# Reordering the last stage of a one-core decode kernel: value products around a layer norm, w_out in two transfers, the last value pieces re-cut

## The chip, the cores and the metric

The kernel runs on one core of a Trainium2 chip. A core has five instruction streams that meet only through semaphores: TensorE (PE, matrix products, with the weight loads shown as PEld), VectorE (DVE), ScalarE (ACT), GpSimd (POOL) and SyncE (SP, which here issues nearly every transfer). The transfers themselves run on 16 DMA engines. The metric is the device time of one execution in microseconds (us); of several executions the median is taken.

## The reference

Four sequences (B = 4) each decode one token. The input row is normalised and modulated, goes through attention over a cache of 4096 keys and values in 32 heads of 128, and then through a gated mixer.

```
mod = silu(c) @ w_mod                       # six groups of 512: sa, ca, ga, sb, cb, gb
h = layernorm(x) * (1 + ca) + sa
q = (h @ wq) in 32 heads of 128
p = softmax(q . k_cache * 128 ** -0.5)      # 4096 keys per head and sequence
x = x + ga * ((p . v_cache) @ wo)
h = layernorm(x) * (1 + cb) + sb
z = gelu(h @ w_in)                          # 1792 columns, two halves of 896
g = w_sp * layernorm(z[second half]) + b_sp # w_sp, b_sp are one number each
x = x + gb * ((z[first half] * g) @ w_out)
```

All inputs are bf16. The two caches together are 256 MiB, and each byte of them is read once, so nearly all of the time is the time of streaming them.

## The kernel before

**Tiles.** The work on the caches is cut into 32 tiles (`NT`), each 4 heads of one sequence: 128 slots (`NJ`) of 128 numbers on each of 128 partitions, 4 MiB of keys and 4 MiB of values. Thirty of them are handled as pairs. The last two (`N0` = 30 and `L` = 31) are single tiles, the last eight heads of the last sequence (`BL` = 3). For each tile the keys are multiplied by the query on DVE (`mult`), summed over the head's dimension on PE and DVE (`reduce_d`, `sum8`, `sum_rest`), and turned into exponentials on ACT (`exps`), which land in `pbd8`. The values then meet these weights on PE (`pv`): groups of four slots are the moving operand, 512 columns, and four groups run side by side in four column strips of the array.

**Buffers and transfers.** Three SBUF buffers of 64 KB per partition (`bufA`, `bufB`, `bufC`) take keys and values in turn. When the keys are through, the weights of the second half of the block are loaded into `bufA`. SP issues, in this order and after the last paired value tile is used: the values of tile `N0` into `bufC` (4 MiB, one transfer), the values of tile `L` into `bufB` in the pieces of `TAIL` (32, 32, 32, 16, 16 slots of 32 KB each), `w_in` in two transfers (`KIN`), `w_out` in one, and the `gb` columns of `w_mod` in two (`KG`, three quarters and one quarter). All are on one hardware queue.

**Order of work.** The order on every engine is the order of the program text (a manual schedule); each engine works through its own list and waits where an operand isn't there. There is no planner that moves work.

**The last stage.** It begins after the loop over the tiles. `turn()` finishes the projection by `wo` of everything but the last eight heads of the last sequence and turns it into columns. DVE then makes `acc` (L777) and `x1` (L779), the row with the attention of all finished heads added. `normed` (L231) is the layer norm over it: a copy, a sum across partitions on PE (`across`, L219), the subtraction, the square, a second `across`, a sum on DVE and ACT's reciprocal root. It has two hooks, `then` and `last`, by which a caller can put PE work behind the first and ahead of the second `across`. Before the change neither is used here.

After it, for the two single tiles: `pv(N0)` (L513, 32 matmuls) makes four partial roots which `o_pick` (L522, L526, four DVE instructions) picks out and adds, `o_cols` (L538) turns into a column, and `o_scale` (L561) scales into `oTp`. `deal` and `dealt` (L640, L652, L658) spread that column for the projection. The last tile `L` goes by pieces, `o_last(L, part)`: pieces 0 and 1 (8 matmuls each) as `pv` does into the other accumulator `ops`, picked by `o_pick(L)`; pieces 2, 3 and 4 slot by slot with the values as stationary operand (L549), into one small accumulator `qps`. `o_first(L)` (L555) adds the picked part of pieces 0 and 1 into the same accumulator. `o_proj4` (L617) and `o_proj` (L607) project the two tiles. The layer norm is then corrected for this one sequence (L801 to L831), and the mixer follows: `gate` (L852), GELU, `zz`, `y` (L877, 28 matmuls by `w_out`), `gb` (L885, 16 matmuls), the mixer's own norm (L890 to L908), the sums of L905 to L918, a transposition (L920) and the output.

Of the kernel before, what the change touches and what calls it, by code (L numbers as in the profile page):

```python
# [9 lines left out]
F32 = mybir.dt.float32  # L10
AF = mybir.ActivationFunctionType
ALU = mybir.AluOpType
AX = mybir.AxisListType
# [3 lines left out]
HP = 8  # L17
KC = 64
RD = 8
TAIL = (32, 32, 32, 16, 16)  # L20
KIN = (slice(0, 2), slice(2, 4))
KG = (slice(0, 3), slice(3, 4))


class Arena:
# [24 lines left out]
def kernel(  # L50
# [16 lines left out]
    nc = tc.nc  # L67
    P = 128
    B, _, D = A_x.shape
# [3 lines left out]
    DJ = D // P  # L73
    NF = F // P
    NH = FH // P
    NJ = SK * HQ // P
    NP = 2 * NJ
    R = P // HQ
    G = 4
    NT = B * H // HQ  # L80
    GP = H // HP - 1
    N0 = NT - 2
# [6 lines left out]
    L = NT - 1  # L89
# [88 lines left out]
    def spread(n, pattern, axis, **sizes):  # L178
# [18 lines left out]
        out=far, in0=half, scalar1=-1.0, scalar2=-NEG, op0=ALU.add, op1=ALU.mult  # L197
    )
    nc.vector.tensor_scalar(
        out=fars, in0=far[:, :, None].to_broadcast([P, 2, R // 2]), scalar1=-1.0, scalar2=None, op0=ALU.mult  # L200
# [30 lines left out]
    def normed(pool, src, name, then=None, last=None):  # L231

        sb = pool.tile([P, B, DJ], F32, name=f"sb_{name}")
        nc.vector.tensor_copy(out=sb, in_=src.rearrange("p j b -> p b j"))
        m = across(sb, inv_d)
        if then:
            then()
        m = summed(pool, m, f"m_{name}")
        xc = pool.tile([P, DJ, B], F32, name=f"xc_{name}")
        nc.vector.tensor_tensor(out=xc, in0=src, in1=bc(m, DJ), op=ALU.subtract)  # L240
        sq = pool.tile([P, B, DJ], F32, name=f"sq_{name}")
        xb = xc.rearrange("p j b -> p b j")
        nc.vector.tensor_tensor(out=sq, in0=xb, in1=xb, op=ALU.mult)
        if last:
            last()
        v = summed(pool, across(sq, inv_d), f"v_{name}")
        rs = pool.tile([P, B], F32, name=f"rs_{name}")
        rsqrt(rs, v, 1.0, eps)
        return xc, rs
# [6 lines left out]
        out=sg, in0=cx, scalar1=-60.0, scalar2=-1.0, op0=ALU.max, op1=ALU.mult  # L256
# [6 lines left out]
    def mod_cols(s0, n, dst):  # L263
# [20 lines left out]
        out=hs, in0=modA[:, DJ:2 * DJ, :], scalar=1.0, in1=xn, op0=ALU.add, op1=ALU.mult  # L284
# [55 lines left out]
    g8 = consts.tile([P, 2, B], F32, name="g8")  # L340
# [163 lines left out]
    def pv(i):  # L504
        n = (NP if pair(i) else NJ) // G
        pv_some(i, 0, n, n)

    def pv_some(i, m0, m1, end):
        pb, vt, rows = (pbd8, bufC, G * HP) if pair(i) else (pbds[:, i % 4], vts[i], G * HQ)
        for m in range(m0, m1):  # L510
            n = slice(m * G, (m + 1) * G)
            g = R * (m % 4)
            nc.tensor.matmul(  # L513
                ops_of(i)[g:g + rows], lhsT=pb[:, n, :], rhs=vt[:, n, :],
                start=(m < 4), stop=(m >= end - 4), tile_position=(0, g),
            )

    def o_pick(i):
        ops = ops_of(i)
        sel = sels[HP if pair(i) else HQ]  # L520
        osb = wk.tile([P, DH], F32, name="osb", bufs=2)
        nc.vector.tensor_scalar(  # L522
            out=osb, in0=ops[:, 0, :], scalar1=sel[:, 0:1], scalar2=None, op0=ALU.mult
        )
        for g in range(1, G):
            nc.vector.scalar_tensor_tensor(  # L526
                out=osb, in0=ops[:, g, :], scalar=sel[:, g:g + 1], in1=osb,
                op0=ALU.mult, op1=ALU.add,
            )
        st[i, "osb"] = osb  # L530

    def o_cols(i):
        if pair(i):
            op = ps_sm([P, P])
            nc.tensor.transpose(op, st.pop((i, "osb")), ident_f)
        else:
            op = ps_sm([P, HQ])
            nc.tensor.matmul(op, lhsT=st.pop((i, "osb")), rhs=sel4, start=True, stop=True)  # L538
        st[i, "op"] = op

    def o_last(i, part):
        n0, n1 = sum(TAIL[:part]), sum(TAIL[:part + 1])
        if part < 2:
            pv_some(i, n0 // G, n1 // G, sum(TAIL[:2]) // G)
            return
        if part == 2:
            st[i, "op"] = psum.tile([P, HQ], F32, name="qps", bufs=1)
        for k in range(n0, n1):
            nc.tensor.matmul(  # L549
                st[i, "op"], lhsT=vts[i][:, k, :], rhs=pbds[:, i % 4, k, :],  # L550
                start=(part == 2 and k == n0), stop=(k == NJ - 1),
            )

    def o_first(i):
        nc.tensor.matmul(st[i, "op"], lhsT=st.pop((i, "osb")), rhs=sel4, start=False, stop=False)  # L555
# [25 lines left out]
    wout_sb = Arena(bufA, 46 * KB, 53 * KB).tile([P, NH, D], BF16)  # L581
    wg_sb = Arena(bufA, 53 * KB, 57 * KB).tile([P, DJ, D], BF16)
    late = Arena(bufA, 57 * KB, 64 * KB)
    tl = Arena(bufC, 32 * KB, 64 * KB)
# [11 lines left out]
    def load_end():  # L596
        win = B_w_in.rearrange("(p j) n -> p j n", p=P)
        for ks in KIN:
            nc.sync.dma_start(out=win_sb[:, ks], in_=win[:, ks])
        nc.sync.dma_start(out=wout_sb, in_=B_w_out.rearrange("(j p) n -> p j n", p=P))  # L600
        for ks in KG:
            nc.sync.dma_start(out=wg_sb[:, ks], in_=wm[:, ks, 5 * D:])

# [44 lines left out]
    def dealt(k, b0=0):  # L648
        pp = st.pop(("pp", k, b0))
        n, nb = pp.shape[1], pp.shape[2]  # L650
        ow = own if n == HP else own[:, 0:n * nb, 0:n]
        nc.vector.tensor_tensor(  # L652
            out=ow, in0=pp.rearrange("p r b h -> p (r b) h"),
            in1=bc(mask8 if n == HP else mask4, n * nb), op=ALU.mult,
        )
        od = late.tile([P, n, nb], BF16, name=f"od{k}{b0}")
        with nc.allow_low_precision("all but one term of each sum are zero"):
            nc.vector.tensor_reduce(  # L658
                out=od.rearrange("p r b -> p (r b)"), in_=ow, axis=AX.X, op=ALU.add
            )  # L660
        st["od", k, b0] = od
# [106 lines left out]
    for i in (N0, L):  # L768
        norm_a(i)
    nc.vector.tensor_reduce(  # L770
        out=sel32, in_=ident_f.rearrange("p (q r) -> p r q", r=R), axis=AX.X, op=ALU.add
# [5 lines left out]
    nc.vector.tensor_tensor(out=acc, in0=wp, in1=gaT, op=ALU.mult)  # L777
    x1 = x1w[:, :, 0:B]
    nc.vector.tensor_tensor(out=x1, in0=acc, in1=xT, op=ALU.add)  # L779
    xc, rs2 = normed(tl, x1, "ln2")  # L780
    pv(N0)
    o_last(L, 0)
    o_pick(N0)
    o_cols(N0)
    o_scale(N0)
    o_last(L, 1)
    deal(GP, slice(BL, B))
    dealt(GP, BL)
    o_pick(L)
    o_last(L, 2)  # L790
    o_first(L)
    wp = ps_sm([P, DJ, 1])
    for j in range(DJ):
        o_proj4(wp, j, slice(BL, B), j == 0)
    o_last(L, 3)
    o_last(L, 4)
    o_scale(L)
    for j in range(DJ):
# [16 lines left out]
        out=x1m, in0=x1[:, :, :, None].to_broadcast([P, DJ, B, HQ]),  # L815
        in1=mask4[:, None, None, :].to_broadcast([P, DJ, B, HQ]), op=ALU.mult,
# [4 lines left out]
        out=nv2, in0=mq2[:, 0:1], scalar=mq2[:, 0:1], in1=mq2[:, 1:2],  # L821
# [7 lines left out]
        out=hl, in0=xs, scalar=mq2[:, 0:1], in1=cbT[:, :, BL], op0=ALU.subtract, op1=ALU.mult  # L829
    )  # L830
    nc.vector.scalar_tensor_tensor(  # L831
        out=hT2[:, :, BL], in0=hl, scalar=rsl, in1=sbT[:, :, BL], op0=ALU.mult, op1=ALU.add
# [3 lines left out]
    for k in range(DJ):  # L836
        nc.tensor.matmul(
            x1r[:, k:P:DJ], lhsT=x1m[:, k].rearrange("p b j -> p (b j)"), rhs=sel32,
            start=True, stop=True,
# [6 lines left out]
    def gate(h, part):  # L846
# [22 lines left out]
    zz = tl.tile([P, NH, 2, B], BF16, name="zz")  # L869
    nc.vector.tensor_tensor(  # L870
        out=zz.rearrange("p f g b -> p g b f"), in0=z1[:, None].to_broadcast([P, 2, B, NH]),
        in1=st3[:, 0:2], op=ALU.mult,
    )
    y = ps_q()[:, 0:DJ * 2 * B].rearrange("p (j g b) -> p j g b", j=DJ, g=2)
    for j in range(DJ):
        for f in range(NH):
            nc.tensor.matmul(  # L877
                y[:, j], lhsT=wout_sb[:, f, j * P:(j + 1) * P], rhs=zz[:, f],
                start=(f == 0), stop=(f == NH - 1),
            )  # L880

    gb = ps_sm([P, DJ, B])
    for k in range(DJ):
        for j in range(DJ):
            nc.tensor.matmul(  # L885
                gb[:, j, :], lhsT=wg_sb[:, k, j * P:(j + 1) * P], rhs=cT[:, k, :],
                start=(k == 0 and j == 0), stop=(k == DJ - 1), skip_group_check=True,
# [3 lines left out]
        out=mq3, in_=ps3.rearrange("p (g b f) -> p g b f", g=2, b=B), axis=AX.X, op=ALU.add  # L891
    )
    rs3 = tl.tile([P, B], F32, name="rs3")
    nc.vector.tensor_tensor(out=rs3, in0=mq3[:, 0], in1=mq3[:, 0], op=ALU.mult)
    nc.vector.scalar_tensor_tensor(
        out=rs3, in0=mq3[:, 1], scalar=LN_EPS, in1=rs3, op0=ALU.add, op1=ALU.subtract
# [5 lines left out]

    yb = y.rearrange("p j g b -> p g b j")
    t3 = tl.tile([P, 3, B, DJ], F32, name="t3")
    nc.vector.tensor_scalar(  # L905
        out=t3[:, 2], in0=yb[:, 0], scalar1=spf[:, 1:2], scalar2=None, op0=ALU.mult
    )
    nc.vector.tensor_tensor(  # L908
        out=g8, in0=g8, in1=rs3[:, None, :].to_broadcast([P, 2, B]), op=ALU.mult
    )  # L910
    nc.vector.tensor_tensor(
        out=t3[:, 0:2], in0=g8[:, :, :, None].to_broadcast([P, 2, B, DJ]), in1=yb, op=ALU.mult
    )
    tt = tl.tile([P, B, DJ], F32, name="tt")
    nc.vector.tensor_reduce(
        out=tt, in_=t3.rearrange("p g b j -> p b j g"), axis=AX.X, op=ALU.add
    )
    nc.vector.tensor_tensor(out=tt, in0=tt, in1=gb.rearrange("p j b -> p b j"), op=ALU.mult)  # L918
    rows = ps_sm([B * DJ, P])
    nc.tensor.transpose(rows, tt.rearrange("p b j -> p (b j)"), ident_f)  # L920
# [33 lines left out]
```

## Time and profile before

| | |
|---|---|
| runs | 665.11, 665.56, 667.5 us; median 665.56 us |
| profiled execution | 667.08 us |
| its span, first to last instruction | 665.0 us |
| DVE busy | 571.1 us (86%) |
| PE matmuls busy | 318.1 us (48%) |
| ACT busy | 171.3 us (26%) |
| POOL busy | 20.0 us (3%) |
| HBM read | 282.73 MB, 425 GB/s over the span |
| mean granted TensorE clock | 0.744 |

The engines work beside each other, so their busy times don't add up to the span. The profile is one execution, and its own time is 2.08 us above its span. Times "at 641.18" are microseconds from the span's start. The chain of waits is the path that set the end: at each step what released it.

### The profile page before, as it was taken

What the parts mean: (1) busy time and instruction counts of PE and PEld (TensorE: products, weight loads), DVE (VectorE), ACT (ScalarE), POOL (GpSimd) and SP (SyncE); (2) the same over time, 40 slices, a digit from 0 to 9 for tenths busy, and PEclk for the clock granted to TensorE, in tenths of its full rate; (3) what the DMA queues carried; (4) which work ended last, traced back from release to release, by engine and by line L of the source; (5) the groups of instructions that cost most, each with busy time, mean ns of one, the idle gap of its engine ahead of it and who ended that gap; (6) DMA issues with size and microseconds to landing.
All of it is one profiled execution on the core that took longest, in us unless ns stands there. A gap on an engine that the chain in (4) does not pass through costs nothing.

```text
span 665.0 us, 5225 instructions
## 1 busy us (share of the span) xinstructions
PE 318.1 (48%) x2134; PEld 137.4 (21%) x2134; DVE 571.1 (86%) x403; ACT 171.3 (26%) x284; POOL 20.0 (3%) x57
## 2 busy tenths in 40 slices
PE   1563543646152364625246461434646243465885
PEld 0221111212021121202112120211212021122344
DVE  3259999989898998989899897989989898999823
ACT  1210606032050604205060410506032050605212
POOL 3000000000000000000000000000000000003100
PEclk9988787857677786767778676787867578787865
DMA  8999999999999999999999999999999999999995
GB/s 362 451 431 430 441 435 442 435 442 435 434 410 441 435 430 441 435 438 439 422 434 442 422 427 441 438 438 442 422 434 435 430 434 439 416 437 430 425 411 205
DMA packets 9356, 283.07 MB, mean 426 GB/s; under 512 B 876, under 2 KB 2804, under 8 KB 3956
## 3 DMA queue, kind: packets, MB, share of 16 engines
q1 hardware_dynamic: 9312, 282.73, 98.6%
q8 instruction: 16, 0.26, 0.1%
q14 instruction: 8, 0.07, 0.0%
q10 hardware_dynamic: 20, 0.01, 0.0%
HBM read 282.73 MB, written 0.00 MB: 425 GB/s over the span
## 4 chain that ended last, share of the span: by engine, by line
DMA 60%; DVE 17%; PE 17%; ACT 4%; issue 1%; POOL 0%; SPq 0%; DVEq 0%; ACTq 0%
DMA bC<-in_A_v_cache_dram 44%; DMA bA<-in_A_k_cache_dram 12%; PE ops L513 10%; DVE bA L384 7%; DVE S L404 5%; ACT pbd L458 3%; PE red L392 3%; DMA bC<-in_w_mod_dram 3%; DVE bB L384 1%; DVE S L415 1%; DMA bC<-in_B_b_sp_dram 1%; PE sm L670 1%; PE qps L319 1%; DVE osb L526 1%; PE sm L311 1%
## 5 line engine op out<-in xcount | busy, mean ns | idle before, releaser
L458 ACT ACTIVATE pbd<-S,nb 32x256 bf16<-32x256 f32 x120 | 154.2, 1519 | 424.9 <-DVE nb L445 423.7
L384 DVE TENSOR_TENSOR bA<-bA,qbp 128x8192 bf16<-128x8192 bf16 x32 | 141.1, 4411 | 25.3 <-DMA bA<-in_A_k_cache_dram 25.3
L392 PE MATMUL red<-bB,ident_bf 128*128 128x512 bf16 x344 | 97.2, 442 | 116.4 <-DVE bB L384 116.3
L392 PE MATMUL red<-bA,ident_bf 128*128 128x512 bf16 x332 | 94.0, 443 | 113.6 <-DVE bA L384 113.4
L392 PEld LDWEIGHTS <-ident_bf 128*128 128x128 bf16 x676 | 73.2, 110 | 344.2 <-issue 176.2
L384 DVE TENSOR_TENSOR bB<-bB,qbp 128x8192 bf16<-128x8192 bf16 x28 | 123.7, 4417 | 15.0 <-DMA bB<-in_A_k_cache_dram 15.0
L513 PE MATMUL ops<-bC,pbd 128*32 128x512 bf16 (+1 forms) x992 | 88.4, 534 | 70.3 <-DMA bC<-in_A_v_cache_dram 65.3
L404 DVE TENSOR_REDUCE S<-bA 128x48 f32<-128x6144 bf16 x15 | 98.1, 6541 | 0.0
L404 DVE TENSOR_REDUCE S<-bB 128x48 f32<-128x6144 bf16 x14 | 91.6, 6542 | 0.0
L513 PEld LDWEIGHTS <-pbd 128*32 128x32 bf16 (+1 forms) x1008 | 37.4, 128 | 119.9 <-issue 65.1
L458 ACT ACTIVATION_READ_ACCUMULATOR pbd<-S,nb 32x1 f32 x120 | 58.6, 489 | 0.0
L415 DVE TENSOR_REDUCE S<-red 128x64 f32<-128x512 f32 x64 | 43.7, 683 | 4.3 <-PE red L392 4.3
L472 POOL TENSOR_TENSOR rsb<-maskd,rs 128x8 f32<-128x8 f32 x15 | 3.9, 260 | 581.3 <-ACT pbd L458 581.3
L384 DVE TENSOR_TENSOR bB<-bB,qbo 128x8192 bf16<-128x8192 bf16 x4 | 17.6, 4412 | 0.0
L526 DVE SCALAR_TENSOR_TENSOR osb<-ops,m,osb 128x128 f32<-128x128 f32 x45 | 15.8, 351 | 1.6
L491 PE MATMUL sm<-rsb,inv_d 128*128 128x32 f32 (+2 forms) x12 | 3.1, 356 | 15.2 <-POOL rsb L472 14.4
L458 ACT ACTIVATE pbd<-S,nM 32x128 bf16<-32x128 f32 x8 | 4.6, 576 | 13.7 <-POOL pbd L718 12.5
L283 DVE SCALAR_TENSOR_TENSOR bC<-sm,bC 128x16 f32<-128x16 f32 x1 | 0.2, 173 | 8.5 <-PE sm L269 8.5
L428 DVE TENSOR_REDUCE mrow<-S 128x1 f32<-128x256 f32 (+1 forms) x17 | 6.9, 404 | 0.6
L631 POOL COPY bA<-ident_bf 128x1024 bf16<-128x1024 bf16 (+1 forms) x2 | 6.5, 3272 | 0.0
L319 PE MATMUL qps<-bC 128*128 128x256 bf16 (+1 forms) x16 | 4.5, 383 | 4.1 <-ACT qbp L329 2.8
L360 DVE COPY modT<-sm 128x48 f32<-128x48 f32 x1 | 0.2, 208 | 7.0 <-PE sm L357 7.0
(160 smaller groups left out, 139.5 us busy)
## 6 DMA issues: line engine op xcount, KB each, us to landing
bA<-in_A_k_cache_dram SPq DMA_DIRECT2D x2, 4096.0 KB, 32.1
bC<-in_A_wq_dram SPq DMA_DIRECT2D x1, 4096.0 KB, 12.2
bB<-in_A_k_cache_dram SPq DMA_DIRECT2D x1, 4096.0 KB, 41.5
bB<-in_A_k_cache_dram SPq DMA_DIRECT2D x2, 2048.0 KB, 40.8
bC<-in_A_v_cache_dram SPq DMA_DIRECT2D x1, 4096.0 KB
bA<-in_A_wo_dram SPq DMA_DIRECT2D x3, 1024.0 KB, 36.8
bB<-in_A_v_cache_dram SPq DMA_DIRECT2D x3, 1024.0 KB, 17.4
bC<-in_w_mod_dram SPq DMA_DIRECT2D x1, 2560.0 KB, 17.9
```

Source lines behind the costliest of these rows:

```text
L311: nc.tensor.matmul(qr[R * q:R * (q + 1)], lhsT=hT[:, k, :], rhs=wq_v[:, k, gs, q, :], start=(k == 0), stop=(k == DJ - 1), tile_position=(0 ...
L319: nc.tensor.matmul(qp[:, 0:npair], lhsT=eb2[k][:, b].rearrange("p k q r -> p (k q r)"), rhs=qrow[:, h, k:2 * npair:2], start=(k == 0), sto ...
L384: nc.vector.tensor_tensor(out=kt, in0=kt, in1=bc(q, KC), op=ALU.mult)
L392: nc.tensor.matmul(red, lhsT=ident_bf, rhs=kt[:, :, m * rd:(m + 1) * rd], start=(m == 0), stop=(m == DH // rd - 1),)
L404: nc.vector.tensor_reduce(out=st[i, "S"][:, n0:NJ], in_=kts[i][:, n0:NJ, :], axis=AX.X, op=ALU.add)
L415: nc.vector.tensor_reduce(out=st[i, "S"][:, kc * KC:kc * KC + on_pe(i, kc)], in_=st.pop((i, "red", kc)), axis=AX.X, op=ALU.add,)
L428: nc.vector.tensor_reduce(out=mrow, in_=S, axis=AX.X, op=ALU.max)
L458: nc.scalar.activation(out=pbd8[r, :, 2 * q + h] if pair(i) else pbds[r, i % 4, :, q], in_=S[r, :], func=AF.Exp, bias=nM[r, h:h + 1], scal ...
L513: nc.tensor.matmul(ops_of(i)[g:g + rows], lhsT=pb[:, n, :], rhs=vt[:, n, :], start=(m < 4), stop=(m >= end - 4), tile_position=(0, g),)
L526: nc.vector.scalar_tensor_tensor(out=osb, in0=ops[:, g, :], scalar=sel[:, g:g + 1], in1=osb, op0=ALU.mult, op1=ALU.add,)
L631: nc.gpsimd.tensor_copy(out=picks[n].rearrange("p r (a u) -> p r a u", a=n), in_=ident_bf.rearrange("p (u r) -> p r u", r=n)[:, :, None, : ...
L670: nc.tensor.matmul(wp, lhsT=od[:, r, :], rhs=wo_sb[:, k * HP + r, :], start=(k == 0 and r == 0), stop=(k == GP - 1 and r == HP - 1),)
```

## The change

Seven edits, all in the last stage or in its transfers.

1. `TAIL` ends in pieces of 24 and 8 slots where it had 16 and 16.
2. `w_out` is loaded in two transfers, the first four and the last three of its seven row blocks (`JW`), where it had one.
3. `pv(N0)` is cut in three: 8 matmuls before the layer norm, 16 behind its first `across` and 8 ahead of its second, where all 32 stood behind the norm.
4. `o_last(L, 1)` stands ahead of `o_cols(N0)`; it stood behind `o_scale(N0)`. `o_last(L, 2)` stands ahead of `o_pick(L)`, where it stood behind it; the two are on different engines.
5. `o_first(L)` stands between `o_last(L, 3)` and `o_last(L, 4)`; it stood before the projection `o_proj4`.
6. The matmuls of `y` go through the first four row blocks of `w_out` for all four groups of columns, and then through the last three, with one start flag for the whole accumulator.
7. At the end the factor `rs3` of the mixer's norm is applied to a sum of two terms, where it was applied to the coefficients `g8`; a three-term reduction becomes two additions.

```diff
-TAIL = (32, 32, 32, 16, 16)
+TAIL = (32, 32, 32, 24, 8)
+JW = (slice(0, 4), slice(4, 7))
...
-        nc.sync.dma_start(out=wout_sb, in_=B_w_out.rearrange("(j p) n -> p j n", p=P))
+        wout = B_w_out.rearrange("(j p) n -> p j n", p=P)
+        for js in JW:
+            nc.sync.dma_start(out=wout_sb[:, js], in_=wout[:, js])
...
-    xc, rs2 = normed(tl, x1, "ln2")
-    pv(N0)
+    nv = NJ // G
+    pv_some(N0, 0, nv // 4, nv)
+    xc, rs2 = normed(
+        tl, x1, "ln2",
+        lambda: pv_some(N0, nv // 4, 3 * nv // 4, nv), lambda: pv_some(N0, 3 * nv // 4, nv, nv),
+    )
     o_last(L, 0)
     o_pick(N0)
+    o_last(L, 1)
     o_cols(N0)
     o_scale(N0)
-    o_last(L, 1)
     deal(GP, slice(BL, B))
     dealt(GP, BL)
+    o_last(L, 2)
     o_pick(L)
-    o_last(L, 2)
-    o_first(L)
     wp = ps_sm([P, DJ, 1])
     for j in range(DJ):
         o_proj4(wp, j, slice(BL, B), j == 0)
     o_last(L, 3)
+    o_first(L)
     o_last(L, 4)
...
-    for j in range(DJ):
-        for f in range(NH):
-            nc.tensor.matmul(
-                y[:, j], lhsT=wout_sb[:, f, j * P:(j + 1) * P], rhs=zz[:, f],
-                start=(f == 0), stop=(f == NH - 1),
-            )
+    for js in JW:
+        for j in range(DJ):
+            for f in range(NH)[js]:
+                nc.tensor.matmul(
+                    y[:, j], lhsT=wout_sb[:, f, j * P:(j + 1) * P], rhs=zz[:, f],
+                    start=(j == 0 and f == 0), stop=(f == NH - 1), skip_group_check=True,
+                )
...
     t3 = tl.tile([P, 3, B, DJ], F32, name="t3")
+    nc.vector.tensor_tensor(
+        out=t3[:, 0:2], in0=g8[:, :, :, None].to_broadcast([P, 2, B, DJ]), in1=yb, op=ALU.mult
+    )
     nc.vector.tensor_scalar(
         out=t3[:, 2], in0=yb[:, 0], scalar1=spf[:, 1:2], scalar2=None, op0=ALU.mult
     )
+    tt = tl.tile([P, B, DJ], F32, name="tt")
+    nc.vector.tensor_tensor(out=tt, in0=t3[:, 0], in1=t3[:, 1], op=ALU.add)
     nc.vector.tensor_tensor(
-        out=g8, in0=g8, in1=rs3[:, None, :].to_broadcast([P, 2, B]), op=ALU.mult
-    )
-    nc.vector.tensor_tensor(
-        out=t3[:, 0:2], in0=g8[:, :, :, None].to_broadcast([P, 2, B, DJ]), in1=yb, op=ALU.mult
-    )
-    tt = tl.tile([P, B, DJ], F32, name="tt")
-    nc.vector.tensor_reduce(
-        out=tt, in_=t3.rearrange("p g b j -> p b j g"), axis=AX.X, op=ALU.add
-    )
+        out=tt, in0=tt, in1=rs3[:, :, None].to_broadcast([P, B, DJ]), op=ALU.mult
+    )
+    nc.vector.tensor_tensor(out=tt, in0=tt, in1=t3[:, 2], op=ALU.add)
     nc.vector.tensor_tensor(out=tt, in0=tt, in1=gb.rearrange("p j b -> p b j"), op=ALU.mult)
```

## The prediction

> **What bounds the kernel now.** I read the page first: busy shares, the chain, and the slices for the transfers. The whole span is a stream from HBM, and then a last stretch that is not.
>
> ```profile
> span 665.0 us, 5225 instructions
> ...
> PE 318.1 (48%) x2134; PEld 137.4 (21%) x2134; DVE 571.1 (86%) x403; ACT 171.3 (26%) x284; POOL 20.0 (3%) x57
> ...
> DMA 60%; DVE 17%; PE 17%; ACT 4%; issue 1%; POOL 0%; SPq 0%; DVEq 0%; ACTq 0%
> ```
>
> DVE is busy for 86%, but transfers hold 60% of the chain. The change touches nothing before 640 us, so I went to the chain of waits there (start, length, what):
>
> ```profile
> 641.18 0.19 DVE bA L777
> ...
> 643.20 0.61 PE sm L219 x2
> 643.80 3.55 PE ops L513 x30
> ...
> 649.03 0.35 PE sm L538 x2
> 649.39 0.54 PE ops L513 x8
> 649.93 0.20 PE sm L640 x4
> ...
> 654.01 0.17 DVE oTp L561
> ...
> 661.77 0.18 DVE bC L918
> ```
>
> From 641.18 on no transfer stands in the chain: it is PE and DVE handing small results to each other, with PE idle in the layer norm (641.15 to 643.73, but for two `across`) and behind each `o_pick`. What these idle stretches are worth is the question. Third, SP's timeline, for the transfers (start, issue time):
>
> ```profile
> 640.69 0.38 SPq L600 DMA_DIRECT2D bA<-in_B_w_out_dram  x1
> 643.13 9.28 SPq L602 DMA_DIRECT2D bA<-in_w_mod_dram  x2
> ```
>
> SP's waits say that L600 waited for the values of `N0` and L602 for the first piece of `L`'s, so these landed at 640.69 and 643.13. `w_out` is the ninth transfer from `N0`'s values on and waits for the first; the tenth waits for the second. Fourth, stretches of the last stage (length, PE, PEld, DVE, ACT, POOL busy, clock, DMA share, GB/s):
>
> ```profile
> 641.42:644.83 3.41, 2.24 (x16) 1.40 (x20) 1.06 (x6) 0.50 (x2) 0.33 (x2) 0.50 1.01 425
> 644.84:648.25 3.41, 3.34 (x32) 0.87 (x24) 0.80 (x3) 0.00 (x0) 0.31 (x2) 0.50 1.01 416
> 648.25:651.66 3.41, 1.89 (x46) 1.38 (x46) 2.13 (x9) 0.00 (x0) 0.00 (x0) 1.00 1.02 419
> ...
> 656.00:658.00 2.00, 1.29 (x32) 1.20 (x33) 0.94 (x5) 1.31 (x3) 0.00 (x0) 0.50 0.61 210
> ```
>
> The queue is full until about 655 and ends near 658.1; the clock is half in two of the first three stretches.
>
> **When data lands.** Value pieces of `L`: the first at 643.13; the fourth was issued at about 627.2 and took 22.2 us, so 649.4. That is 2.5 MiB in 6.27 us, 2.5 us a MiB: piece 1 at 645.6, piece 2 at 648.1, and everything at 650.6. `w_in` 631.0 + 23.8 = 654.8. `w_mod`'s first piece 643.13 + 15.1 = 658.2; its second, 128 KB at some 200 GB/s, 658.9. `w_out` lies between 654.8 and 658.2, 896 of 1280 KB: 657.2, and its first 512 KB 656.2. These are estimates but for the landings that a row shows.
>
> **A, `pv(N0)` around the norm.** 32 matmuls move ahead; they issue no transfer, and their values are there (640.69) before the turned projection ends (641.15). Four run in 0.43 us at half clock (32 took 3.59). Eight go into 641.05 to 641.95, while DVE makes `acc`, `x1` and the copy, ready at 641.84: the first `across` starts at 641.95 in place of 641.90. The other 24 follow from 642.5 and take 2.57, so 645.1 with 0.17 to drain. The price: the second `across` stands behind them, and DVE's sum of it stands ahead of `o_pick(N0)`; 645.2 + 0.61 + 0.05 + 0.18, and `o_pick` begins at 646.05, ends 1.52 later at 647.57, where it ended at 648.90. ACT's root and POOL's L810 wait 2 us longer, but L811's result is first used at 657.4. Gain 1.33 at half clock. If the clock returns to full at 644.83, the rest of `pv` is over at 645.07, `across` takes 0.3 (at full clock L491 does two such sums in 0.58) and `o_pick` ends at 647.14: gain 1.76.
>
> Whether it returns is open. The flips of the clock that I narrowed down (638.0, 648.25, 651.66) are whole multiples of 3.41 apart; a stretch with 3.25 of 3.41 us of 512-column matmuls (504.89 to 508.30) was followed by full clock, one with 2.19 (566.33 to 569.74) was not. The new 641.42 to 644.83 has about 2.8. It lies as near to one as to the other, so I keep both ends. The Trainium skill ("TensorE: Matmul & The Clock Gate", Part 1) says the same of windows: they are free-running, 3413 ns long, and a busy one brings the full rate. By that page alone the full-clock values here and below would stand, and the whole gain would be 2.4 to 2.7; going by half clock it is 2.2. The flips agree with its length; no row shows its threshold.
>
> **B, `o_last(L, 1)` ahead of `o_cols(N0)`.** Now the wait from `o_pick`'s end to the end of `deal` is 648.90 to 650.13, 1.23, because `deal` stands behind eight matmuls (0.54). They move into `o_pick`'s time (PE is free from about 645.8, piece 1 is there at 645.6). What is left: 0.13 + 0.35 + 0.05 + 0.17 + 0.04 + 0.22 = 0.96, or 1.20 if `o_cols` runs at half clock (L555, the same shape, took 0.59). Gain 0.27 or 0.03. `deal` ends at 648.10 or 648.77. What now waits behind piece 1 on PE is `o_cols`, and behind that all of the chain: a piece 2 us late would cost directly.
>
> **C, `o_first` late, pieces 24 and 8.** Now from `deal`'s end to L561: 3.88 (650.13 to 654.01), because `o_first` waits for `o_pick(L)` with 16 + 32 short matmuls behind it. After: piece 2 (0.92), `o_proj4` (0.52), 24 of piece 3 (0.65), `o_first` (0.59), 8 of piece 4 (0.32 with the drain), 0.04: 3.0. `o_pick(L)` ends 1.83 after `deal`, inside that. At half clock L561 starts at 648.77 + 3.0 = 651.8, gain 2.2. At full clock `deal` is so early that piece 3 (24 slots, landing at 649.4 + 0.6 = 650.0) holds PE: 650.0 + 0.65 + 0.59 (or 0.35) + 0.32 + 0.04 = 651.6 (651.35), gain 2.4 (2.65). Without the cut at 24 the wait would be no shorter: all slots land at 650.6 in both.
>
> **D, the tail.** L801 to L870 move as a block. `y` would start at 659.74 - 2.4 = 657.34: its first blocks are there at 656.2, the rest at 657.2 and used 0.5 later. `gb`'s last four matmuls need 658.9, and the product by it stands at 661.77 - 2.4 = 659.37: covered by about 0.3. If this cover goes, the end is 658.9 + 0.2 and the gain is limited to 2.7. The new sums: from `y` ready (660.65) five DVE steps, 0.22 + 0.26 + three of 0.20, end at 661.73 before the last product, where it starts at 661.77 now. Removing `g8`'s product and the reduction saves 0.4 behind `rs3`, but the two terms of `y` have moved behind `y`. 0.0, between 0.1 either way. The start flag and the loop order of `y` cost nothing: 28 matmuls before and after.
>
> **E, `w_out` in two.** One more issue on SP (0.38), ahead of `w_mod`'s. The second half waits for piece 0 (643.13), `w_mod` for pieces 1 and 2 (645.6, 648.1); but its issue took 6.59 and 2.65 us and ended at 649.7 and 652.4, so these waits lie inside it. 0, if the issue's end is set by the queue draining; the rivals price the other case.
>
> **Sum.** 2.2 at half clock to 2.7 at full: I take 2.4, since both ends depend on a threshold that no row gives. Span 665.0 to 662.6; the profiled execution 667.08 to 664.7. That execution lies 1.5 above the median, 665.56, and from the median it is 663.2.
>
> **Rivals.**
> *Transfers take it back.* The last rows of `w_mod`, in 1 KB rows, went at 210 GB/s, not 405. If both parts of `w_out` (917 kB, also 1 KB rows) go at 210, everything behind them lands 4.4 - 2.3 = 2.1 us later, `gb` ends at about 661.2, and only 0.5 us is left: 665.0. Value pieces 1 us late (B, C) would give 664.2. For it: 0.91 and 0.61 of DMA share where the last pieces are alone. Against: two value pieces of 512 KB ran at a share of 1.0. The Trainium skill ("DMA: Bandwidth & Descriptors", Rules for kernel authors) asks for at least 1 MiB a transfer, which speaks against cutting `w_out`; the 512 KB pieces here don't bear that out.
> *Slower: SP holds the last weights.* `w_out`'s second part has 384 rows of 1 KB, as the `w_mod` piece has whose issue took 6.59 us. If that is the issue's own price, SP passes `w_out` at 649.7, the `w_mod` pieces at 656.3 and 659.0, and the last lands between 2.3 (the output's issue to the span's end) and 8.5 us (658.2 - 649.7) later: 661.3 to 667.5, the middle 664.4. It decides from 661.6 on, where the product by `gb` waits longer than now; the middle costs 2.8 us: 668.4. Against: `w_out`'s 896 rows took 0.38.
> *More.* Full clock, and value pieces and weights landing about 1 us earlier than estimated, so that nothing waits for them: 1.76 + 0.27 + (3.88 - 2.80) + 0.1 = 3.2 us, 662.4. For it: most landings are estimates. Against: the queue is full to 655, and its order stays.
> *The norm is not overlapped.* If `N0`'s values land 1 us later, PE waits at 641.15 for them, and A keeps 0.5: 664.2; the first rival's neighbour, counted with it.
>
> **How the numbers follow.** Forecast 0.60; transfers take it back 0.20; slower 0.06; more 0.14. 0.5% is 3.3 us, about what a measurement of this kernel can tell from no change. Even "more" stays just under it, so faster by over 0.5% takes the runs' scatter (2.4 us between the three) as well: half of "more" and somewhat over a tenth of the forecast, 0.07 + 0.07 = 0.14. Slower, 0.06; within, 0.80. Range 661.9 ("more", with 0.5 for the scatter) to 665.6 (gain lost whole); the forecast's own is 662.5 to 663.8.
>
> **What would show it.** A: L513 from `bC` begins near 641.1, `o_pick(N0)` near 646. B: `deal` near 648.1 to 648.8. C: L561's second near 651.6, `o_first` between the L549 groups. D: L918 near 659.4 and no wait on a transfer. E: `w_mod`'s issue ends near 652. Wrong if PE waits for a value piece ahead of `o_cols`, if `gb` waits for `w_mod`, or if the chain before 641 us differs.

## The result, and the profile after

In 22 executions of each kernel the changed one takes 664.45 us in the median and the one before 667.09 us; the ratio is 0.997, with an interval of 0.9962 to 0.9978. A second comparison of the two gave 664.33 against 667.1 us, ratio 0.9968 (0.9958 to 0.9978). That is about 2.0 us by the ratios and 2.7 us by the medians, inside the range given and within 0.5%. (One execution of the changed kernel took 922 us, with PE busy for 757 us instead of 317 at a recorded clock of 1.00; it is not in the ratio, and the profile below is that of the second comparison, whose profiled execution took 664.29 us.)

The page of the changed kernel, against that of before: three instructions more, the same busy times within 1 us, a span shorter by 2.5 us.

```profile
span 662.5 us, 5228 instructions
...
PE 317.3 (48%) x2134; PEld 136.7 (21%) x2134; DVE 570.9 (86%) x404; ACT 171.4 (26%) x284; POOL 20.0 (3%) x57
...
DMA 60%; DVE 24%; PE 12%; ACT 2%; issue 1%; SPq 0%; DVEq 0%; ACTq 0%
```

The chain of waits of the changed kernel from 636 us on (start, length, what). Line numbers behind the edit are higher by 1 to 8:

```profile
627.08 22.91 DMA bB<-in_A_v_cache_dram
649.99 0.05 issue
650.04 0.80 PE qps L550 x24
650.84 0.43 PE qps L556 x2
651.26 0.23 PE qps L550 x8
651.49 0.03 issue
651.51 0.17 DVE oTp L562
...
659.18 0.18 DVE bC L925
```

Before, no transfer stood in this chain behind 641 us. Now it begins with one: the value piece of 24 slots, landing at 650.0, for which PE waits. The timeline of PE in the same execution shows the steps between:

```profile
641.05 1.03 PE L514 MATMUL ops<-bC,pbd 128*16 128x512 bf16 x8
642.01 0.61 PE L220 MATMUL sm<-bC,inv_d 128*128 128x16 f32 x2
642.55 2.54 PE L514 MATMUL ops<-bC,pbd 128*16 128x512 bf16 x24
645.02 0.40 PE L220 MATMUL sm<-bC,inv_d 128*128 128x16 f32 x2
645.35 1.04 PE L514 MATMUL ops<-bB,pbd 128*16 128x512 bf16 x16
647.20 0.36 PE L539 MATMUL sm<-m,osb 128*128 128x4 f32 x2 [0.81 <-DVE osb L527]
647.81 0.24 PE L643 MATMUL sm<-oTp,bA 128*128 128x4 bf16 x4 [0.25 <-DVE oTp L562]
...
650.04 0.80 PE L550 MATMUL qps<-pbd,bB 128*128 128x4 bf16 x24 [0.36 <-DMA bB<-in_A_v_cache_dram]
...
658.35 0.59 PE L893 MATMUL sm<-cT,bA 128*128 128x4 bf16 x16 [0.21 <-DMA bA<-in_w_mod_dram]
```

The value product surrounds both sums of the norm; the second sum takes 0.40 us, not 0.61, because the clock has come back. The stretches show it (length, busy PE, PEld, DVE, ACT, POOL, clock, DMA share, GB/s):

```profile
641.43:644.84 3.41, 3.41 (x34) 1.19 (x26) 0.89 (x5) 0.00 (x0) 0.22 (x1) 0.51 1.01 424
644.84:648.25 3.41, 2.25 (x36) 1.26 (x29) 1.82 (x7) 0.50 (x2) 0.42 (x2) 0.99 1.01 415
648.25:651.66 3.41, 2.87 (x82) 2.73 (x82) 1.64 (x7) 0.00 (x0) 0.00 (x0) 0.50 1.01 420
```

Full clock comes one stretch earlier than before, and goes one stretch earlier. SP's timeline, last:

```profile
640.80 4.86 SPq L603 DMA_DIRECT2D bA<-in_B_w_out_dram  x2
645.70 6.82 SPq L605 DMA_DIRECT2D bA<-in_w_mod_dram  x2
```

The last issue ends at 652.52, where it ended at 652.41.

### The profile page after: what moved, and what is told of

Same layout as the page of the kernel before. It is cut to its first block, busy times and chain, and to the rows that moved or that the text cites. A ratio compares the mean times of both kernels' runs of the same rounds, so it can differ in the third digit from the quotient of the medians.

```text
span 920.7 us, 5228 instructions
## 1 busy us (share of the span) xinstructions
PE 757.3 (82%) x2134; PEld 235.7 (26%) x2134; DVE 572.2 (62%) x404; ACT 171.2 (19%) x284; POOL 21.6 (2%) x57
## 4 chain that ended last, share of the span: by engine, by line
PE 66%; DVE 19%; issue 6%; DMA 5%; ACT 4%; SPq 0%; POOL 0%; ACTq 0%; DVEq 0%; POOLq 0%
PE red L393 43%; PE ops L514 19%; DVE S L405 10%; DVE bB L385 4%; ACT pbd L459 3%; DVE bA L385 3%; DMA bC<-in_w_mod_dram 2%; DMA bB<-in_A_v_cache_dram 2%; DMA bA<-in_w_mod_dram 1%; DVE S L416 1%; PE sm L312 1%; PE qps L320 1%; PE sm L348 0%; PE sm L536 0%; PE sm L492 0%
## 5 line engine op out<-in xcount | busy, mean ns | idle before, releaser
L393 PE MATMUL red<-bB,ident_bf 128*128 128x512 bf16 x344 | 257.0, 999 | 67.7 <-DVE bB L385 67.7
L393 PE MATMUL red<-bA,ident_bf 128*128 128x512 bf16 x332 | 257.2, 1032 | 64.4 <-DVE bA L385 64.4
L393 PEld LDWEIGHTS <-ident_bf 128*128 128x128 bf16 x676 | 134.3, 201 | 497.1 <-issue 496.9
L514 PE MATMUL ops<-bC,pbd 128*32 128x512 bf16 (+1 forms) x992 | 186.6, 1005 | 0.7 <-ACT pbd L459 0.7
L514 PEld LDWEIGHTS <-pbd 128*32 128x32 bf16 (+1 forms) x1008 | 64.7, 191 | 115.7 <-issue 112.3
L570 DVE TENSOR_REDUCE oU<-sm 128x8 f32<-128x128 f32 x15 | 4.4, 291 | 65.5 <-PE sm L536 65.5
L673 PE MATMUL sm<-bA 128*4 128x512 bf16 x24 | 14.2, 819 | 0.0
L523 DVE TENSOR_SCALAR osb<-ops,m 128x128 f32<-128x128 f32 x15 | 5.2, 345 | 7.4 <-PE ops L514 7.4
L536 PE MATMUL sm<-ident_f,osb 128*128 128x128 f32 x15 | 8.6, 570 | 0.0
```

The lines of the kernel that those rows point to most:

```text
L393: nc.tensor.matmul(red, lhsT=ident_bf, rhs=kt[:, :, m * rd:(m + 1) * rd], start=(m == 0), stop=(m == DH // rd - 1),)
L514: nc.tensor.matmul(ops_of(i)[g:g + rows], lhsT=pb[:, n, :], rhs=vt[:, n, :], start=(m < 4), stop=(m >= end - 4), tile_position=(0, g),)
L673: nc.tensor.matmul(wp, lhsT=od[:, r, :], rhs=wo_sb[:, k * HP + r, :], start=(k == 0 and r == 0), stop=(k == GP - 1 and r == HP - 1),)
```

## The experiments

**The changed kernel again, and with parts undone.** Theory: the prediction's steps A, B and C, with transfers hidden. Rival: the transfers take the gain back. The first kernel is the changed one as it is.

> The changed kernel whole, for an undisturbed profile. Theory (the prediction's): a gain of 2.0 to 2.7 us, ratio 0.996 to 0.997; in the profile o_pick of tile 30 begins about 0.9 to 1.7 us after the turned projection's x1 plus 3.5, that is 1.3 us (half clock) to 1.8 us (full clock) earlier than before when both are counted from L777; from o_pick's end to the end of deal 0.96 to 1.20 us (before 1.23); from deal's end to the second scaling of oTp 3.0 to 3.5 us (before 3.88); the last product by gb waits for no transfer. Rival (the transfers take it back): PE waits for a value piece ahead of o_cols or for the last w_mod piece ahead of gb, and the steps before it are shorter by 3 us or more.

Measured: 664.33 us, as above. From L777 to `o_pick`'s end it takes 5.89 us (641.16 to 647.05) where it took 7.71; from there to the end of `deal` 1.00; from there to the second scaling of `oTp` 3.46. The last three instructions of `o_pick(N0)`, in the kernel before and then in the changed one, on which the first number rests:

```profile
647.77 1.12 DVE L526 SCALAR_TENSOR_TENSOR osb<-ops,selg,osb 128x128 f32<-128x128 f32 x3
...
645.93 1.12 DVE L527 SCALAR_TENSOR_TENSOR osb<-ops,selg,osb 128x128 f32<-128x128 f32 x3
```

The theory holds with the full-clock numbers. The rival does not: PE does wait for two transfers, but not where the rival put the waits or for as long. It waits 0.36 us for the piece of 24, behind `o_cols` and not ahead of it, and 0.21 us for `w_mod`; and the product by `gb` starts at 659.18, behind the sums that end at 659.07, not behind `gb` (658.94).

Edit 3 alone, on the kernel before:

```diff
-    xc, rs2 = normed(tl, x1, "ln2")
-    pv(N0)
+    nv = NJ // G
+    pv_some(N0, 0, nv // 4, nv)
+    xc, rs2 = normed(
+        tl, x1, "ln2",
+        lambda: pv_some(N0, nv // 4, 3 * nv // 4, nv), lambda: pv_some(N0, 3 * nv // 4, nv, nv),
+    )
```

> The kernel before with edit 3 alone (the value product of tile 30 cut in three around the norm). Theory: step A alone, 1.3 to 1.8 us faster, ratio 0.9973 to 0.998. Rival (A is cancelled by what stands behind it, o_last(L, 1) or the short matmuls): 0 to 0.5 us faster, ratio 0.9993 to 1.0.

Measured: 665.69 us, ratio 0.9984 (0.9973 to 0.9994), 1.1 us. In the profile `o_pick` ends 6.13 us behind L777, 1.58 earlier than before, and the second scaling of `oTp` and the last product are earlier by 1.57 and 1.56: nothing behind it takes A back. But L777 itself began at 642.04, not at 641.18. That was not expected of a kernel that is the same up to there, and it comes back below.

Edits 1 and 5 undone in the changed kernel:

```diff
-TAIL = (32, 32, 32, 24, 8)
+TAIL = (32, 32, 32, 16, 16)
...
     o_pick(L)
+    o_first(L)
...
     o_last(L, 3)
-    o_first(L)
     o_last(L, 4)
```

> The changed kernel with edits 1 and 5 undone (pieces of 16 and 16, o_first ahead of the projection). Theory: step C goes, 0.6 to 0.9 us slower than the changed kernel, still 1.3 to 2.0 us faster than before, ratio 0.997 to 0.998. Rival (the value pieces' landing sets this stretch): no difference to the changed kernel, within 0.2 us.

Measured: 664.84 us, ratio 0.9976 (0.9965 to 0.9987), 0.5 us above the changed kernel, a little less than expected and with overlapping intervals. Five of its 12 executions lie at 665.6 to 666.5, where four of 33 of the changed kernel lie above 665.5. In the profile `deal`'s end to the scaling is 3.86 us, as before (3.88), against 3.46: step C is worth 0.4 net of the wait for the piece. And here the turned projection ended at 639.4, so PE waited:

```profile
640.62 1.03 PE L514 MATMUL ops<-bC,pbd 128*16 128x512 bf16 x8 [1.22 <-DMA bC<-in_A_v_cache_dram]
```

Edits 2 and 6 undone (`w_out` in one transfer):

```diff
-JW = (slice(0, 4), slice(4, 7))
+JW = (slice(0, 7),)
```

> The changed kernel with edits 2 and 6 undone (w_out in one transfer, y in its old loop order). Theory: no difference to the changed kernel, within 0.3 us, either way. Rival (the two transfers of w_out delay the last weights): 0.5 us or more faster than the changed kernel. A third reading (y waited for w_out and the split relieved it): 0.3 to 0.8 us slower than the changed kernel.

Measured: 664.51 us, ratio 0.9976 (0.9964 to 0.9987), above the changed kernel by 0.2 us in the medians and 0.5 by the ratios, and not separated from it. The profile shows the third reading, at its lower edge:

```profile
657.25 0.91 PE L885 MATMUL qps<-bC,bA 128*128 128x8 bf16 x28 [0.21 <-DMA bA<-in_B_w_out_dram]
```

`y` waits for `w_out`, which lands at 657.25, and from the second scaling of `oTp` to the last product it takes 7.98 us, against 7.67 with the split. So two transfers are worth 0.3 us in this execution, and cost nothing. That they would delay `w_mod` is not borne out.

**What scatters.** The times of the kernel before fall into two groups. Of 96 executions measured beside these kernels, 34 lie below 666.0, 51 above 666.6 and 11 between; the changed kernel lies at 664.0 to 664.7 in 28 of 33. The profiles name a cause: the sums of tile `L`'s keys (16 matmuls, L392). In the profile before:

```profile
617.66 0.62 PE L491 MATMUL sm<-rsb,inv_d 128*128 128x24 f32 x2 [2.36 <-POOL rsb L472]
618.10 0.39 PE L640 MATMUL sm<-oTp,bA 128*128 128x32 bf16 x8
618.33 4.88 PE L392 MATMUL red<-bB,ident_bf 128*128 128x512 bf16 x16
```

They take 4.88 us there, 5.30 with edit 3 alone, and 3.61 where edits 1 and 5 are undone. All profiles of this document but that of 922 us fit: in the five with 3.61 us L777 (or the same instruction under its later number) begins at 639.3 to 639.7, in the eight with 4.85 to 5.30 us at 641.0 to 642.0. Where edits 1 and 5 are undone the clock stays full from 609.0 to 636.3; in the profile before it is half from 617.5 to 621, behind a stretch in which PE worked only 1.18 of 3.41 us. The flips fall elsewhere in the two executions, so the stretches do too: of the three from 609.0 to 619.23, the least busy has 1.82 us (from 615.82 on), and the clock is kept. The Trainium skill ("TensorE: Matmul & The Clock Gate", Part 1) says that the windows by which the clock is set run freely and don't begin with the kernel, so that where the clock changes varies from execution to execution. The changes seen here, at 617.5, at 619.0 or not at all, agree. To test it, PE is kept busy in that stretch:

```diff
         sum_rest(i)
+        if i == L - 1:
+            keep = ps_q()
+            for m in range(8):
+                nc.tensor.matmul(
+                    keep, lhsT=ident_bf, rhs=ident_bf[:, None, :].to_broadcast([P, 4, P]),
+                    start=True, stop=True,
+                )
```

> The kernel before with eight extra 128x512 matmuls on PE (into an accumulator that nobody reads) behind the key sums of tile 30, where PE is idle from 615.3 to 617.6 in the profile before. They only keep PE busy. Theory (the clock of the stretch from 617.5 to 621 decides when the turned projection ends, and this makes the two groups of times of the kernel before, 665 to 666 and 666.6 to 667.7): the later group goes, the median falls by 1.3 to 1.8 us to 665.2 to 665.6, ratio about 0.998, and L777 (here some lines further down) begins near 639.5, not 641.2. Rival (the scatter comes from the transfers or from outside): the same two groups, ratio 1.0.

> The changed kernel with the same eight extra matmuls. Theory: the turned projection ends 1.7 us earlier as well, but the value product of tile 30 now waits 1.0 to 1.3 us for its values (they land at 640.6 to 640.8 whatever PE does), so the time stays that of the changed kernel, 664.2 to 664.5, and the gain over the kernel before with the extra matmuls is 0.8 to 1.3 us only. Rival (the chain is PE's and DVE's throughout): 1.3 to 1.8 us faster than the changed kernel, about 662.8.

Measured: the kernel before with the extra matmuls takes 665.82 us, ratio 0.9987 (0.9977 to 0.9998), and its slowest of 12 executions takes 666.16, where the kernel before beside it reached 668.5. 13 of the 26 beside it lie above that, so the later group goes. L777's place begins at 639.46 (expected 639.5). By the medians (666.03 and 665.82) the gain is only 0.2 us, and the median is higher than expected: eight of the 12 lie at 665.7 to 666.2. The profile, of one of these (665.74), shows one reason: its clock stayed half from 637.0 to the end, and `o_cols` and `o_last(L, 1)` took 0.56 and 1.03 us, not 0.35 and 0.61. Whether that holds for the other seven is not shown. The changed kernel with the extra matmuls takes 664.22 us, as without them, and its timeline shows why:

```profile
617.73 3.61 PE L393 MATMUL red<-bB,ident_bf 128*128 128x512 bf16 x16
...
640.54 1.03 PE L514 MATMUL ops<-bC,pbd 128*16 128x512 bf16 x8 [1.27 <-DMA bC<-in_A_v_cache_dram]
...
649.82 0.80 PE L550 MATMUL qps<-pbd,bB 128*128 128x4 bf16 x24 [0.34 <-DMA bB<-in_A_v_cache_dram]
```

Arriving 1.8 us earlier (L777's place at 639.32, not 641.16), it waits 1.27 us for tile 30's values and again for the piece, and ends as before. The gain of the change is 1.6 us in the medians where both are kept warm. The rival, a chain of PE and DVE throughout, would have given 662.8.

**The single edits.** Edit 7 undone (the sums of L903 to L917 as they were):

> The changed kernel with edit 7 undone (rs3 applied to the coefficients, three-term reduction). Theory (step D): no difference to the changed kernel, within 0.15 us. Rival (the shorter path behind rs3 is worth its 0.3 to 0.4): 0.3 us or more slower.

Measured: 664.47 us. From the second scaling of `oTp` to the last product 7.77 us, against 7.67: edit 7 is worth 0.10.

Edit 1 alone undone, `TAIL` at (32, 32, 32, 16, 16) with the late root:

> The changed kernel with edit 1 alone undone (value pieces of 16 and 16, o_first still late). In the changed kernel PE waits 0.36 us for the piece of 24 slots. Theory: the piece of 16 is there at 649.4, that wait goes, the last 16 slots run behind o_first from 650.6; the second scaling of oTp is 0.2 to 0.3 us earlier counted from the landing of the values of tile 30, and the end gains 0 to 0.2 us, since the first w_mod piece holds gb. Rival (the cut at 24 is what the late root needs): 0.2 us or more slower.

Measured: 664.12 us, ratio 0.9967 (0.9953 to 0.998). From the landing of tile 30's values (640.85) to the second scaling 10.50 us, against 10.70 and 10.76 in the two executions of the 24-slot cut that also waited for these values (edit 7 undone, and kept warm). As expected. The last product stands at 659.02, against 659.18 in the changed kernel and 658.97 with it kept warm. The cut at 24 is not what brings the gain.

The first half of edit 4 undone:

```diff
-    o_last(L, 1)
     o_cols(N0)
     o_scale(N0)
+    o_last(L, 1)
```

> The changed kernel with the first half of edit 4 undone (o_last(L, 1) again between o_scale(N0) and deal). Theory: deal ends 0.2 to 0.5 us later counted from o_pick's end (step B), but the piece of 24 slots lands at 650.0 and PE waited 0.34 to 0.36 us for it, so the second scaling of oTp moves by 0 to 0.15 us only and the time by no more. Rival (B counts in full): 0.25 to 0.5 us slower than the changed kernel.

Measured: 664.57 us in only six executions, ratio 0.9967 (0.9955 to 0.998). In its profile the projection ended late (641.90), `o_pick`'s end to `deal`'s end took 1.23 us instead of 1.00, and the piece of 24 was there when PE came to it. Whether it costs in the median stays open: 0.24 us more than the changed kernel in another comparison lies between the two readings.

Edit 3 alone undone:

```diff
-    nv = NJ // G
-    pv_some(N0, 0, nv // 4, nv)
-    xc, rs2 = normed(
-        tl, x1, "ln2",
-        lambda: pv_some(N0, nv // 4, 3 * nv // 4, nv), lambda: pv_some(N0, 3 * nv // 4, nv, nv),
-    )
+    xc, rs2 = normed(tl, x1, "ln2")
+    pv(N0)
```

> The changed kernel with edit 3 alone undone (the whole value product of tile 30 behind the norm). Theory: step A counts where the turned projection ends late (641 to 642): there 1.3 to 1.8 us of the gain go, less what the wait for the piece of 24 gives back, so 1.0 to 1.5 us slower than the changed kernel, and the two groups of times of the kernel before come back, 664.3 to 664.9 and 665.3 to 666.0. Where it ends early (639.5) the norm is over before the values land, and A is worth 0.2 or less. Rival (A counts the same in all executions): one group, about 665.6 to 666.

Measured: 665.61 us, ratio 0.998 (0.9968 to 0.9991). Four of 12 executions lie at 664.37 to 664.88, one at 665.33, six at 665.5 to 665.96, one at 667.33: the groups are back. In the profile the projection ended late (L777's place at 641.57) and the second scaling followed 11.37 us behind, against 10.35: A is worth 1.0 net of the wait that it runs into. So edit 3 is needed to take the late arrivals in, but it is not enough: alone on the kernel before its times still run from 664.61 to 666.66, and without edits 1 and 5 from 664.09 to 666.43. The profiles suggest how they act together, which no run tests by itself: an early arrival waits for tile 30's values (1.2 to 1.3 us at 640.5 to 640.9), and a late one no longer waits for the piece of 24 (0.36 us in the changed kernel, nothing at 641.90 in the run of edit 4).

**Two further versions.** One with three edits: `o_pick` ahead of the norm's second sum, `o_first` ahead of the piece of 24, and `w_out` in runs of 7 KB, for which `w_in`'s columns are taken with a step of seven:

```diff
+    def pick_early():
+        pv_some(N0, 3 * nv // 4, nv, nv)
+        o_last(L, 0)
+        o_pick(N0)
...
-        lambda: pv_some(N0, nv // 4, 3 * nv // 4, nv), lambda: pv_some(N0, 3 * nv // 4, nv, nv),
+        lambda: pv_some(N0, nv // 4, 3 * nv // 4, nv), pick_early,
     )
-    o_last(L, 0)
-    o_pick(N0)
...
+    o_first(L)
     o_last(L, 3)
-    o_first(L)
...
-        wout = B_w_out.rearrange("(j p) n -> p j n", p=P)
+        wout = B_w_out.rearrange("(p j) n -> p j n", p=P)
...
-            n0 = (h * NH + f) * P
+            n0 = h * FH + f
-                    zs[h][:, f, :], lhsT=win_sb[:, k, n0:n0 + P], rhs=hT2[:, k, :],
+                    zs[h][:, f, :], lhsT=win_sb[:, k, n0:n0 + (P - 1) * NH + 1:NH], rhs=hT2[:, k, :],
```

> A further version: the changed kernel with o_pick(N0) ahead of the norm's second sum on DVE (and the second across behind o_last(L, 0) on PE), o_first between the projection and the piece of 24, and w_out's rows taken so that each partition reads one run of 7 KB (w_in's columns are picked with a step of seven to match). Theory: o_pick ends 0.4 to 0.5 us earlier, o_first lies in the wait for the piece of 24, only that piece and the last eight slots follow its landing, and the second scaling of oTp is 0.2 to 0.3 us earlier counted from the landing of tile 30's values; the w_mod pieces land earlier, so gb waits for nothing; the time is 663.9 to 664.1. Rival (strided weight loads cost more than that): gate takes more than its 1.63 us and the time is 664.4 or more.

Measured: 665.71 us, ratio 0.9985 (0.9975 to 0.9996). The rival is right; the groups of instructions of this kernel's `gate` (L863), busy time and mean of one behind the count:

```profile
L863 PEld LDWEIGHTS <-bA 128*128 128x128 bf16 x56 | 3.1, 153 | 0.7 <-issue 0.6
L863 PE MATMUL red<-bC,bA 128*128 128x4 bf16 x56 | 3.1, 192 | 0.7 <-DVE bC L842 0.7
```

`gate` takes 3.10 us where it took 1.63, both at a clock of 0.50, and from the second scaling to the last product it is 9.12 us, against 7.67. The reordering did what was expected of it: the second scaling comes 10.04 us behind L777's place, against 10.35. And though SP's issue of `w_mod` fell from 6.82 to 2.77 us, the transfers ended at about 658 as in the other profiles, so the length of that issue delayed nothing. The last version leaves the strides out and keeps `pick_early`, with pieces of 16 and 16:

> The further version without the strided weights: the changed kernel with o_pick(N0) ahead of the norm's second sum on DVE, the second across behind o_last(L, 0) on PE, and value pieces of 16 and 16 with the late root. Theory: o_pick begins 0.2 to 0.45 us earlier counted from x1, the value pieces' landing sets the second scaling of oTp, 10.4 to 10.6 us after tile 30's values (10.7 in the changed kernel where PE waits for them), and the time is 663.9 to 664.2, the same in nearly all executions. Rival (nothing is left to win ahead of the pieces): 664.3, as the changed kernel.

Measured: 664.09 us, ratio 0.9965 (0.9953 to 0.9978), all seven executions between 663.79 and 664.37. Its median is the lowest of all, 0.03 us below the one with pieces of 16 and 16 alone and 0.2 to 0.4 below the changed kernel, which no interval here separates. In its profile the second scaling comes at 651.09, and now `gb` is late:

```profile
658.17 0.63 PE L897 MATMUL sm<-cT,bA 128*128 128x4 bf16 x16 [0.43 <-DMA bA<-in_w_mod_dram]
...
658.84 0.17 DVE L929 TENSOR_TENSOR bC<-bC,sm 128x16 f32<-128x16 f32 x1 [0.16 <-PE sm L897]
```

## Why the prediction was right, and where it was not

**The sum.** Predicted 2.2 to 2.7 us, taken 2.4; the steps A to D measure 1.82 + 0.23 + 0.42 + 0.09 = 2.56, the two profiled spans differ by 2.5, the interval of the ratio is 1.5 to 2.5 us, and the two medians of the long comparison differ by 2.6. The predicted time, 663.2, is 1.25 us below the measured one. The step that failed there is the level: the three times of the kernel before that were shown have a median of 665.56, and two of the three lie in its earlier group; over 22 executions it is 667.09. The profiled execution, 667.08, lay where most do, and from it the prediction had 664.7; I took the median of three over it. That the size fits as well as it does is in part luck: both profiled executions begin this stretch late and at the same place (641.18 and 641.16). Where both kernels are kept warm, and so begin it early, the gain is 1.6 us, below the 2.2 of the forecast's lower end.

**A.** Predicted 1.33 at half clock or 1.76 at full; 1.82 measured, 1.58 with edit 3 alone, where the clock came back during the second sum (646.2) and not ahead of it. The stretch from 641.43, with PE busy for all of its 3.41 us, was followed by full clock; whether it would be had been left open.

**B.** Predicted 0.27 or 0.03 with 0.96 or 1.20 left; 0.23 and 1.00.

**C.** Predicted at full clock: PE held at 650.0 by the piece of 24, the scaling at 651.35 to 651.6. It waited until 650.04, and the scaling came at 651.51. The estimates of the landings were good to 0.15 us: 650.0 (650.04), `w_out` 657.2 (657.25 where it was whole), `w_mod`'s first piece 658.2 (658.35). Wrong in one sentence: I wrote that without the cut at 24 the wait would be no shorter. With 16 and 16 the first of the two pieces no longer waits, `o_first` fills the time to the second, and the scaling comes 0.2 us earlier.

**D.** Predicted 0.0, between 0.1 either way; 0.09 from the scaling to the last product, all of it edit 7's by the run without it (0.10). "No wait on a transfer" was wrong in the letter, and `gb` waiting for `w_mod` stood on the prediction's own list of signs of being wrong: it waits 0.21, in the shadow of DVE's sums. The cover for `gb` was given as about 0.3 us; 658.94 to 659.07 is 0.13, and the last version uses it up.

**E.** Predicted 0 for SP, and the last issue ended at 652.52 (predicted near 652). What E and D left out: without the split `y` would have waited for `w_out` (0.21 us seen), so edits 2 and 6 earn 0.3 us once A to C have moved `y` forward.

**The rivals.** "More" did not come: the clock returned, but the landings were where they were estimated and held PE. The slower one (SP holding the last weights to 659) did not happen: the second part of `w_out` and both parts of `w_mod` were through at 652.5. Of "the transfers take it back", the 2.1 us for slow rows did not come, but the value pieces and tile 30's values do set the end now. "The norm is not overlapped" was priced with late values; it happened with early work instead, in four of the profiles (1.2 to 1.3 us of waiting at 640.5 to 640.9), and cost nothing, because the time saved ahead of it was as long. What the prediction did not see is that the place where its chain begins, 641.18, is not fixed: it lies between 639.3 and 642.0, by the clock some 20 us earlier, and the gain is larger where it is late (1.6 us where both kernels are kept warm, 2.5 between the two spans that begin late).

## What to carry to other kernels

Where a kernel's times fall into two groups, look upstream for instructions that take longer in one profile than in another, as the 16 key sums do here, and read a change's gain in both groups. Work moved ahead pays until a landing holds it; list the landings beside the chain before adding up the steps, and the sum stops where they say. Counting from the same event in both traces (here L777 and the second scaling) gave steps to 0.1 us, where the times of whole executions could not separate 0.3 us.

## What the runs showed of the hardware

The same 16 matmuls took 3.61 us at full clock and 4.85 to 5.30 us where the clock was half for part of them. Eight more matmuls in an idle stretch made the kernel before faster by 0.9 us by the ratio (0.9987) and by 0.2 in the medians, and took away its latest executions. Weight loads that take every seventh column took about twice as long: 56 of them with their matmuls 3.10 us, not 1.63, at a clock of 0.50 in both. And the issue of the same two `w_mod` transfers on SP took 9.28, 6.82 or 2.77 us, with what stood ahead of it, while their data ended at 658.0 to 658.3 each time.
